# A rebuilt opening for a delta-rule attention and feed-forward kernel on one core

## The chip, the cores and the metric

The kernel runs on one core of a Trainium2 chip. Its engines are TensorE (PE in the profile, with PEld for the loading of its stationary operand), VectorE (DVE), ScalarE (ACT), GpSimd (POOL) and SyncE (SP), which issues most of the transfers. Each engine works through its own instruction stream in order and waits on semaphores for the others. The metric is the device time of one execution in microseconds; lower is better.

## The reference

Two blocks follow each other. The first is a delta-rule attention over 4 batches of 8 heads, 768 positions and 48 dimensions, with normalized keys:

```python
k_n = k / (np.linalg.norm(k, axis=-1, keepdims=True) + 1e-06)
state = np.zeros((B, H, D, D)); y = np.zeros_like(q)
for t in range(S):
    kt, vt, bt = k_n[:, :, t], v[:, :, t], beta[:, :, t, None]
    y[:, :, t] = np.einsum('bhd,bhde->bhe', q[:, :, t], state)
    v_old = np.einsum('bhde,bhd->bhe', state, kt)
    state = state + bt[:, :, :, None] * np.einsum('bhd,bhe->bhde', kt, vt - v_old)
```

Its output, 3072 tokens of 384 numbers, goes through a feed-forward block:

```python
h = x @ w_in                                     # 384 x 2048
g = np.maximum(h, 0.0) + alpha * np.minimum(h, 0.0)
out = g @ w_out                                  # 2048 x 384
```

All is float32.

## The kernel before, in words

The sequence is cut into 12 chunks of 64 positions. A step `n` is one chunk for one pair of batches, so there are 24 steps; steps 0 and 1 are the first chunk. Within a chunk the recurrence becomes a triangular system: a Gram matrix of the keys, weighted by beta, is inverted, and the inverse is applied to the values less what the state already gives. `attention` or the bursts of later steps do this in small matrix products; the feed-forward products of earlier chunks (`ffn_in`, L943, and `ffn_out`) are woven between them by `weave`, which places pieces by their shares. There is no scheduler: the order on every engine is the order of the Python code (`manual_schedule`). PSUM is held as three double banks (`p_pair`), which `ps_big` and `ps_one` hand out in rotation, and two single ones (`p_ffn`, from `ps_ffn`).

The opening is the part from L1528 to the first feed-forward product. It is written out by hand:

- *Loads.* `load_early` brings keys to one of three buffers (`ke`; the fourth step uses `kl`), `load_q`, `load_v` and `load_late` queries, values and a second copy of the keys, all as DMAs on SP's queue but three of the first, which are on ACT's. `fetch_in` issues DMAs of pieces of `w_in`, 512 KB each, to staging space in `w_out` and `space_out`. `begin_in` makes two ACT instructions of each piece (L226, L227) and `convert` two DVE instructions (L236, L241), which turn it into the form that the products read.
- *Key preparation, steps 0 to 3.* `squares` (square on ACT, sum on DVE), `weigh` (root and a small bias on ACT, reciprocal on DVE, two small products on GpSimd, L373 and L374), `flips` (four transpositions on PE, L384, and an eviction to `k_t` by ACT, L410), `grams` (16 small products on PE, L436; two weighted evictions on DVE, L442; and `keep`, which copies half of the rows to `same`: on GpSimd, L485, for steps 0 to 2, and half on DVE, L487, and half on ACT, L489, for step 3). `betas` transposes beta, `slopes` the feed-forward slopes (L310), `queries` multiplies queries by keys (L1417).
- *The first inversion.* `turn_in` transposes `same` into `block` on DVE (L501, 4 instructions). `eliminate_small(0)` then inverts the two 16x16 diagonal blocks of every 32x32 block. It first multiplies `block` by the mask `inside` (L563), which keeps what is strictly above the diagonal; `inside` is made of `ones` (GpSimd, L268 and L269) by a cast on ACT (L1553). Then follow 14 pairs of DVE instructions (L569, L575). `back` transposes the results to `turned` (2 instructions), to `inverse` (4) and to the rest of `turned` (2).
- *Meanwhile* ACT clears tiles (`zeros`, L327 and L329) and begins four weight pieces; PE runs `busy(8)`: eight products of 128x512 (L1407) whose result nobody reads. `busy` takes a PSUM bank and repeats such a product; each shows as two records in the profile.
- *The crossing.* `cross` fills in the off-diagonal 16x16 blocks for a range of blocks: products of `edge` with `turned` (L605), an ACT copy to `half_way` (L610), products with `inverse` (L615 for the upper, L622 for the lower), DVE additions (L629 and L631). In `first_chunk` it runs once over the 16 blocks of steps 0 and 1, with `busy` products inside and behind it.
- *The rest of `first_chunk`.* `scale_v` and `mask` (DVE, L749 and L1425) stand inside the crossing. `place` puts the results into `diag` and `inv` (DVE or ACT, L650 and L654); `between_1` and `between_2` (L721 and L734, with evictions L726 and L741) complete the 64x64 inverse; `solve` (L800, L804), `outputs` (L813, L818) and `to_ffn` (L852, L854) end in the operand of the first L943. Three transpositions of later keys (`flipped`) stand between, and 12 conversion steps.

`second_pair` follows: it does the crossing for steps 2 and 3, in two halves and with products of `ffn_in(0)` between.

Of the kernel before, what the change touches and what calls it, by code (L numbers as in the profile page):

```python
# [32 lines left out]
C = 64  # L33
HB = 32
W_IN_P = 512
BUSY = 8
EARLY = 8
FIRST = 6
LATE = 16
# [4 lines left out]
def kernel(  # L44
# [219 lines left out]
    for t in range(2):  # L264
        nc.gpsimd.tensor_copy(out=above[half(t)], in_=upper[half(t), half(t)])

    ones = work.tile([128, HB, HB], FP32, name="ones", tag="turned", bufs=1)
    nc.gpsimd.memset(ones, 0.0)  # L268
    nc.gpsimd.affine_select(  # L269
        out=ones, in_=ones, compare_op=ALU.is_ge, fill=1.0, base=0,  # L270
        pattern=[[1, HB], [-1, HB]], channel_multiplier=0,
    )
    inside_ = const.tile([128, HB * (HB + 1)], S8, name="inside")
    inside = inside_[:, 0 : HB * HB].rearrange("p (r c) -> p r c", c=HB)

    which = const.tile([128, 2], FP32, name="which")
    nc.gpsimd.memset(which, 0.0)
    for t in range(2):
# [42 lines left out]

    right = [const.tile([128, H + 1, HB], FP32, name=f"right{i}") for i in range(EARLY)]

    def zeros():

        for t in right:
            nc.scalar.memzero(t[:, 0])  # L327
        for t in mid + diag + inv + state:
            nc.scalar.memzero(t)  # L329


    stats, k_t, q_t, a_t = {}, {}, {}, {}
# [97 lines left out]
    def grams(n, p=None):  # L430

        if n >= N:
            return []
        p = region(p, G * C, g=G)
        for g, a, t in quarters():
            nc.tensor.matmul(  # L436
                p[half(t), a, g], k_t[n][dims(a), g, half(t)], k_t[n][dims(a), g, half(t)]
            )
        w = stats[n][1][:, 0:2, :, None].to_broadcast([128, 2, G, HB])

        def weighted(dst, cols):
            nc.vector.tensor_tensor(  # L442
                out=dst.rearrange("p (a g) i -> p a g i", a=2), in0=p[:, :, :, cols], in1=w,
                op=ALU.mult,
            )
# [33 lines left out]
    def keep(n):  # L479

        m, j = n // NJ, n % NJ
        for t in range(2):
            own = slice(64 * t + HB, 64 * t + C)
            if n < FIRST + NJ and n != NJ - 1:
                nc.gpsimd.tensor_copy(out=same[m][own, j], in_=right[n % EARLY][own, 1:])  # L485
            elif n < NJ and t == 0:
                nc.vector.tensor_copy(out=same[m][own, j], in_=right[n % EARLY][own, 1:])  # L487
            else:
                nc.scalar.copy(same[m][own, j], right[n % EARLY][own, 1:])  # L489
        if (m, j) == (0, NJ - 1):  # L490
            for _ in turn_in(m):
                pass
# [98 lines left out]
    def quad(i):  # L591
        return slice(HB * i, HB * i + HB)

    def cross(m, bs, edge, half_way, aside=None):


        def let(b, every):
            if aside is not None and b % every == every - 1:
                aside()

        n = bs.stop - bs.start
        p = ps_one()[:, 0 : n * LB].rearrange("p (b i) -> p b i", i=LB)
        for b in range(n):
            for i in range(4):
                nc.tensor.matmul(  # L605
                    p[quad(i), b], edge[quad(i), bs.start + b],
                    turned[m][quad(i), bs.start + b, 0:LB],
                )
            let(b, 4)
        nc.scalar.copy(half_way[:, bs, 0:LB], p)  # L610
        yield
        p = ps_big()[:, :, 0 : n * LB].rearrange("p w (b i) -> p w b i", i=LB)
        for b in range(n):
            for i in (0, 2):
                nc.tensor.matmul(  # L615
                    p[quad(i), 1, b], inverse[m][quad(i), bs.start + b],
                    half_way[quad(i), bs.start + b, 0:LB],
                )
            let(b, 8)
        for b in range(n):  # L620
            for i in range(4):
                nc.tensor.matmul(  # L622
                    p[quad(i), 0, b], half_way[quad(i), bs.start + b],
                    inverse[m][quad(i), bs.start + b, LB:HB],
                )
            let(b, 4)
        for i in (0, 2):
            y = turned[m][quad(i), bs, 0:LB]
            nc.vector.tensor_tensor(out=y, in0=y, in1=p[quad(i), 1], op=ALU.add)  # L629
# [772 lines left out]
    def busy(n, p=None):  # L1402

        p = ps_one() if p is None else p
        while n > 0:
            x = p[:, 0 : int(512 * min(n, 1))]
            nc.tensor.matmul(  # L1407
                x, ident, k_late[0].rearrange("p h d -> p (h d)")[:, 0 : x.shape[-1]]
            )
            n -= 1  # L1410

# [20 lines left out]
    def first_chunk(mask, convert):  # L1432

        both = (0, 1)
        ahead[0] = n_in

        waits, pause = iter([0.5] * 2), []
        middle = cross(
            0, slice(0, 2 * H), edge, half_way, lambda: pause and busy(next(waits, 0), pause[0])
        )  # L1440
# [11 lines left out]
        place(0, (0,))  # L1452
        place(1, (0,), True)
        for i in both:
            place(i, (1,), True)
            now(between_1(i))
        keys = flipped(NJ, ps_ffn())
        convert(2)
# [6 lines left out]
        norms(NJ)  # L1465
        for i in both:
            now(through_state(i))
            now(solve(i))
        now(flipped(NJ + 1, ps_ffn()))
        for i in both:  # L1470
            now(outputs(i))
        convert(4)
        fetch_in(n_in + 4)
        load_early(NJ + NKE)
        for i in both:
            to_ffn(i, ps_ffn())
        now(flipped(NJ + 2, ps_one()))
        ahead[0] = FT * DM
        convert(4)
        norms(NJ + 1)  # L1480

    def statics(first, last):
# [45 lines left out]
    load_early(NKE)  # L1528
    for n in range(2):
        load_q(n)  # L1530
        load_v(n)
    load_late(0)
    nc.sync.dma_start(out=al_sb, in_=moe_alpha.rearrange("(f p) -> f p", p=128))
    fetch_in(n_in)
    squares(0)
    flips(0, N)
    betas()
    fetch_in(n_in + 2)
    squares(1)
    now(weigh(0))  # L1540
    for n in range(1, NJ):
        if n == 1:
            gram = grams(0)
        flips(n, N)
        if n > 1:
            gram = grams(n - 1)
        now(gram)
        if n + 1 < NJ:
            squares(n + 1)
        now(weigh(n))  # L1550
        load_early(n + NKE)
    now(grams(NJ - 1))
    nc.scalar.copy(inside, ones)  # L1553
    edges(0, edge)
    load_late(1)
    load_v(2)
    slopes()
    for i in range(2):
        flips(N, i)
    for i in range(2):  # L1560
        load_q(i + 2)
    mask = queries()
    nc.scalar.mul(minus, above, -1.0)
    zeros()
# [274 lines left out]
```

## Time and profile before

| | us |
|---|---|
| runs | 658.03, 663.54, 664.56 |
| median | 663.54 |
| span of the profiled execution (the page gives no other time of it) | 658.5 |
| PE busy | 642.4 (98%) |
| DVE busy | 490.4 (74%) |
| ACT busy | 263.9 (40%) |
| POOL busy | 93.4 (14%) |
| first feed-forward product (L943) starts | 48.84 |

Times in the profile count from the first instruction. A line of the timeline has start, length, engine, line, operation, tiles written and read, shapes, the number of instructions merged into it and, in brackets, the idle time of the engine before it and what ended that. The chain that ended last is read in order of time: at each moment the instruction, or the wait ("issue" when the profile shows nothing that was waited for), that the end depended on. A line of the table by stretches gives the stretch, its length, the busy time and number of instructions of PE, PEld, DVE, ACT and POOL, the granted TensorE clock (1.00 is full), the share of DMA engines busy and GB/s.

### The profile page before, as it was taken

The page shows a single profiled execution, that of the slowest core. Times are in us where ns is not written, and L with a number is a line of the kernel's source. Part 1 is how long each engine was busy: PE and PEld are TensorE (multiplying, and loading weights), DVE is VectorE, ACT ScalarE, POOL GpSimd, SP SyncE. Part 2 cuts the span into 40 slices and gives each one's busy share as a digit, 9 for nine tenths or more (in the row PEclk, how much of TensorE's full clock was granted, in tenths as well). Part 3 has the DMA queues.
Part 4 walks back from the last instruction along what each step waited for, and adds up shares of the span by engine and source line. Part 5 has one row for each costly group of instructions (what it writes and reads, how often), then busy time and mean ns, then how long its engine had stood idle before and what let it go on. Part 6 is the DMA issues. An engine that isn't in the chain of part 4 may idle for free.

```text
span 658.5 us, 22123 instructions
## 1 busy us (share of the span) xinstructions
PE 642.4 (98%) x9545; PEld 567.5 (86%) x9545; DVE 490.4 (74%) x1180; ACT 263.9 (40%) x621; POOL 93.4 (14%) x201
## 2 busy tenths in 40 slices
PE   5999999999999999999999999999999999999997
PEld 4477888657788988988988988988989999999997
DVE  3975899977999779658869758868868658567383
ACT  4855755344453443143253242133245245042140
POOL 6000211010000000000000000000035044052260
PEclk9999999999999999999999999999999999999999
DMA  7946745311422122122111111111111210100000
GB/s 124 293 97 158 194 121 148 73 36 37 75 54 50 34 54 38 25 59 41 26 43 33 26 39 36 26 42 33 26 44 32 45 32 2 31 8 2 24 1 25
DMA packets 111154, 37.72 MB, mean 57 GB/s; under 512 B 104224, under 2 KB 107440, under 8 KB 111056
## 3 DMA queue, kind: packets, MB, share of 16 engines
q1 hardware_dynamic: 109184, 35.81, 24.5%
q8 instruction: 75, 1.23, 0.8%
q10 hardware_dynamic: 1872, 0.49, 0.4%
q14 instruction: 23, 0.19, 0.1%
HBM read 31.56 MB, written 4.72 MB: 55 GB/s over the span
## 4 chain that ended last, share of the span: by engine, by line
PE 91%; DVE 5%; ACT 1%; issue 1%; POOL 1%; DMA 1%; SPq 0%; POOLq 0%; ACTq 0%; DVEq 0%
PE p_ffn L943 24%; PE p_ffn L1008 17%; PE p_more L1260 8%; PE p_ffn L986 5%; PE p_more L1176 5%; PE p_ffn L1166 3%; PE p_ffn L1260 3%; PE p_pair L775 2%; PE p_pair L384 2%; PE p_ffn L1171 2%; PE p_pair L686 2%; PE p_pair L800 2%; PE p_pair L813 2%; PE p_pair L1407 2%; PE p_pair L436 2%; PE p_pair L760 1%
## 5 line engine op out<-in xcount | busy, mean ns | idle before, releaser
L943 PE MATMUL p_ffn<-xt,w_in 128*128 128x256 f32 x768 | 176.1, 383 | 0.6 <-DVE act L955 0.5
L943 PEld LDWEIGHTS p_ffn<-xt,w_in 128*128 128x128 f32 x768 | 142.4, 190 | 21.2 <-issue 1.5
L955 DVE SCALAR_TENSOR_TENSOR act<-act,al_t,p_ffn 128x256 f32<-128x256 f32 x112 | 48.7, 476 | 26.5 <-ACT act L953 26.5
L953 ACT ACTIVATE act<-p_ffn 128x512 f32<-128x512 f32 x56 | 33.2, 594 | 79.4 <-PE p_ffn L943 79.2
L534 DVE TENSOR_TENSOR block<-block,prod 128x30 f32<-128x30 f32 (+9 forms) x150 | 49.8, 332 | 5.2
L1200 POOL TENSOR_TENSOR k_t<-k_t 128x128 f32<-128x128 f32 (+1 forms) x48 | 29.3, 610 | 167.1 <-ACT k_t L1195 164.6
L528 DVE TENSOR_TENSOR prod<-block 128x30 f32<-128x30 f32 (+9 forms) x150 | 48.8, 326 | 1.4
L1008 PE MATMUL p_ffn<-w_out,act 128*128 128x192 f32 x288 | 49.6, 328 | 0.0
L854 ACT COPY xt<-p_pair 128x384 f32<-128x384 f32 x22 | 10.4, 478 | 91.1 <-PE p_pair L852 77.3
L1008 PEld LDWEIGHTS p_ffn<-w_out,act 128*128 128x128 f32 x288 | 46.5, 190 | 0.3
L373 POOL TENSOR_TENSOR beta_t<-beta_t,rec 128x8 f32<-128x8 f32 x24 | 6.3, 265 | 283.9 <-DVE rec L371 268.6
L1200 POOL TENSOR_TENSOR block<-block 128x128 f32<-128x128 f32 (+1 forms) x48 | 27.9, 582 | 17.2 <-ACT block L1195 14.7
L1166 PE MATMUL p_ffn<-xt,w_in 128*128 128x256 f32 x96 | 28.7, 381 | 0.5 <-DVE o_sb L1028 0.5
L785 DVE TENSOR_TENSOR r<-v_raw,p_pair 64x192 f32<-64x192 f32 (+1 forms) x66 | 23.3, 353 | 2.3 <-PE p_pair L775 1.2
L698 ACT COPY inv<-p_pair 32x256 f32<-32x256 f32 x40 | 14.4, 361 | 25.0 <-DVE u L804 24.2
L352 DVE TENSOR_REDUCE norm<-ksq 128x8 f32<-128x384 f32 x24 | 13.0, 548 | 14.3 <-ACT ksq L348 14.3
L804 DVE TENSOR_TENSOR u<-p_pair,wgt 128x384 f32<-128x384 f32 x24 | 13.2, 556 | 14.0 <-PE p_pair L686 14.0
L1028 DVE TENSOR_TENSOR o_sb<-u,p_ffn 128x192 f32<-128x192 f32 x24 | 8.0, 352 | 20.4 <-PE p_ffn L1008 20.0
L1214 DVE SCALAR_TENSOR_TENSOR act<-block,al_t,act 128x256 f32<-128x256 f32 x32 | 19.1, 638 | 5.3 <-ACT block L1210 5.2
L764 ACT COPY y<-p_pair 128x384 f32<-128x384 f32 x22 | 10.4, 478 | 30.2 <-PE p_pair L760 26.1
L1260 PE MATMUL p_more<-w_out,act 128*128 128x192 f32 x128 | 21.8, 329 | 0.0
L1195 ACT COPY k_t<-p_more 128x512 f32<-128x512 f32 x16 | 9.4, 585 | 31.1 <-PE p_more L1176 26.4
(228 smaller groups left out, 1422.1 us busy)
## 6 DMA issues: line engine op xcount, KB each, us to landing
w_out<-in_moe_w_in_dram SPq DMA_DIRECT2D x10, 512.0 KB, 5.5
qp<-in_q_dram SPq DMA_DIRECT2D x48, 96.0 KB, 3.0
v_raw<-in_v_dram SPq DMA_DIRECT2D x48, 96.0 KB, 2.9
kl<-in_k_dram SPq DMA_DIRECT2D x96, 48.0 KB, 2.5
out_dram<-o_sb SPq DMA_DIRECT2D x90, 48.0 KB, 1.6
space_out<-in_moe_w_out_dram SPq DMA_DIRECT2D x11, 384.0 KB, 4.1
ke<-in_k_dram SPq DMA_DIRECT2D x43, 96.0 KB, 3.3
w_out<-in_moe_w_out_dram SPq DMA_DIRECT2D x5, 384.0 KB, 4.0
```

What stands on the lines that cost most here:

```text
L528: nc.vector.tensor_tensor(out=prod, in0=r[:, 0:j, j : j + 1].to_broadcast([128, j, n]), in1=r[:, j : j + 1, j + 1 : HB].to_broadcast([128, ...
L534: nc.vector.tensor_tensor(out=r[:, 0:j, j + 1 : HB], in0=r[:, 0:j, j + 1 : HB], in1=prod, op=ALU.add)
L785: nc.vector.tensor_tensor(out=r[to, a], in0=v_in[to, a], in1=p[own, a, :, 0:D], op=ALU.subtract)
L943: nc.tensor.matmul(p_h[:, i], w_in[:, t, (f + i) * 128 : (f + i + 1) * 128], xt[:, t], start=(t == 0), stop=(t == KT - 1),)
L953: nc.scalar.activation(g, p_h, ACT.Relu, scale=-1.0)
L955: nc.vector.scalar_tensor_tensor(out=g[:, i], in0=g[:, i], scalar=al_t[:, f + i : f + i + 1], in1=p_h[:, i], op0=ALU.mult, op1=ALU.add,)
L986: nc.tensor.matmul(p_o[u], gs[f // 2][:, f % 2, u * 128 : (u + 1) * 128], w_out[:, f], start=(f == 0), stop=(f == FT - 1),)
L1008: nc.tensor.matmul(p, x(i), w(i), start=(i == 0), stop=(i == FP - 1))
L1166: nc.tensor.matmul(p[:, f * 256 : f * 256 + 256], w(2, f), xt[:, 2], start=True, stop=False)
L1176: nc.tensor.matmul(q[:, j], a, b, start=True, stop=True)
L1200: nc.gpsimd.tensor_tensor(out=dst, in0=a, in1=b, op=ALU.add)
L1260: nc.tensor.matmul(p, x(i), w(i), start=(i == 0), stop=(i == FP - 1))
```

## The change

Only the opening is changed; from `second_pair` on the code is the same.

- The order of key preparation: weights (`weigh`) of a step come ahead of the evictions of the Gram products of the steps before it, and the transpositions write to the single banks.
- Six products of 128 columns (`WARM`) start PE's stream.
- Key loads 4 to 6 are issued ahead of the weight pieces, the values and late keys behind them.
- `zeros` runs on GpSimd: 12 clears early, 4 more after key preparation.
- The mask `inside` and its product are gone; 15 GpSimd clears of the lower triangles take their place. `keep` uses GpSimd for steps 0 and 1, DVE and ACT for 2 and 3.
- The three later key transpositions move ahead of the crossing, among fillers of 7, 5, 3 and 1 products; between them ACT begins four weight pieces. The filler reads a transposed key tile (112 rows) in place of a late key tile (128 rows).
- The first crossing runs in two halves, without fillers; the upper additions come ahead of the lower products. Value scaling and masks move behind it, and the 12 conversion steps are split 2, 4 and 6.

```diff
-BUSY = 8
+WARM = 6
...
-    def zeros():
-
-        for t in right:
-            nc.scalar.memzero(t[:, 0])
-        for t in mid + diag + inv + state:
-            nc.scalar.memzero(t)
+    def zeros(tiles):
+
+        for t in tiles:
+            nc.gpsimd.memset(t, 0.0)
...
-            if n < FIRST + NJ and n != NJ - 1:
+            if n < 2 or NJ <= n < FIRST + NJ:
...
-        nc.vector.tensor_tensor(out=x, in0=x, in1=own_blocks(inside_), op=ALU.mult)
+        for j in range(1, LB):
+            nc.gpsimd.memset(x[:, :, j, 0:j], 0.0)
...
+        if apart:
+            upper_half()
+            yield
         for b in range(n):
             for i in range(4):
                 nc.tensor.matmul(
                     p[quad(i), 0, b], half_way[quad(i), bs.start + b],
                     inverse[m][quad(i), bs.start + b, LB:HB],
                 )
-            let(b, 4)
...
-        next(middle)
-        pause.append(ps_one())
-        busy(1, pause[0])
+        halves = [cross(0, slice(i * H, i * H + H), edge, half_way, True) for i in both]
+        for h in halves:
+            next(h)
         begin_in(6)
+        for h in halves:
+            next(h)
+        for i in both:
+            place(i, (0,))
+        for h in halves:
+            next(h)
+        for i in both:
+            place(i, (1,), True)
         for i in both:
             scale_v(i)
-            mask(i)
+        for i in both:
+            now(between_1(i))
         convert(2)
         fetch_in(n_in + 3)
-        next(middle)
-        busy(1.25)
...
         for i in both:
             place(i, (2,))
             now(between_2(i))
-        now(keys)
+            mask(i)
...
+    for _ in range(WARM):
+        nc.tensor.matmul(big[0][:, 0, 0:128], ident, ident)
+    zeros([t[:, 0] for t in right] + mid + diag)
+    squared(0)
+    norms(0)
+    now(flipped(0, ps_ffn()))
+    rest = [weigh(0)]
+    squared(1)
+    now(flipped(1, ps_ffn()))
+    load_early(1 + NKE)
+    norms(1)
+    betas()
+    now(rest[0])
+    rest = weigh(1)
+    gram = {0: grams(0)}
+    squared(2)
+    now(rest)
+    norms(2)
+    now(flipped(2, ps_ffn()))
...
+    fetch_in(n_in + 2)
+    now(gram[0][2:])
+    now(gram[1][2:])
+    now(gram[2][:2])
+    gram[3] = grams(3)
+    now(gram[2][2:])
+    now(gram[3][:2])
+    now(gram[3][2:])
...
+    zeros(inv + state)
...
-    busy(BUSY)
-    begin_in(4)
+    for i in range(3):
+        busy(7 - 2 * i)
+        now(flipped(NJ + i, ps_one()))
+        begin_in(i + 2)
+    busy(1)
     for _ in eliminate_small(0):
         pass
```

More of the change, by code (lines that the diff above doesn't have):

```diff
@@ L265 @@
         nc.gpsimd.tensor_copy(out=above[half(t)], in_=upper[half(t), half(t)])
[L267 to L274, printed above, removed]
     which = const.tile([128, 2], FP32, name="which")
@@ L438, in grams @@
             )
-        w = stats[n][1][:, 0:2, :, None].to_broadcast([128, 2, G, HB])
         def weighted(dst, cols):
+            w = stats[n][1][:, 0:2, :, None].to_broadcast([128, 2, G, HB])
             nc.vector.tensor_tensor(
@@ L592, in quad, with cross @@
         return slice(HB * i, HB * i + HB)
[L594 to L599, printed above, removed]
+    def cross(m, bs, edge, half_way, apart=False):
         n = bs.stop - bs.start
@@ L618, in cross, with upper_half @@
                 )
-            let(b, 8)
+        def upper_half():
+            for i in (0, 2):
+                y = turned[m][quad(i), bs, 0:LB]
+                nc.vector.tensor_tensor(out=y, in0=y, in1=p[quad(i), 1], op=ALU.add)
+        if apart:
+            upper_half()
+            yield
         for b in range(n):
@@ L625, in cross @@
                 )
[L626 to L629, printed above, removed]
+        if not apart:
+            upper_half()
         y = inverse[m][:, bs, LB:HB]
@@ L1405, in busy @@
         while n > 0:
-            x = p[:, 0 : int(512 * min(n, 1))]
             nc.tensor.matmul(
-                x, ident, k_late[0].rearrange("p h d -> p (h d)")[:, 0 : x.shape[-1]]
+                p, ident[0:ROWS], k_t[0].rearrange("p g i -> p (g i)")[0:ROWS]
             )
@@ L1435, in first_chunk @@
         ahead[0] = n_in
[L1437 to L1440, printed above, removed]
-        next(middle)
-        pause.append(ps_one())
-        busy(1, pause[0])
-        begin_in(6)
+        halves = [cross(0, slice(i * H, i * H + H), edge, half_way, True) for i in both]
+        for h in halves:
+            next(h)
+        begin_in(6)
+        for h in halves:
[6 more added lines that the diff above has]
+            place(i, (1,), True)
         for i in both:
             scale_v(i)
-            mask(i)
+        for i in both:
+            now(between_1(i))
         convert(2)
         fetch_in(n_in + 3)
-        next(middle)
-        busy(1.25)
[L1452 to L1458, printed above, removed]
         for i in both:
@@ L1461, in first_chunk @@
             now(between_2(i))
-        now(keys)
+            mask(i)
         for i in both:
             squared(NJ + i)
-        norms(NJ)
         for i in both:
@@ L1468, in first_chunk @@
             now(solve(i))
-        now(flipped(NJ + 1, ps_ffn()))
         for i in both:
@@ L1473, in first_chunk @@
         fetch_in(n_in + 4)
+        norms(NJ)
         load_early(NJ + NKE)
@@ L1476, in first_chunk @@
             to_ffn(i, ps_ffn())
-        now(flipped(NJ + 2, ps_one()))
         ahead[0] = FT * DM
-        convert(4)
+        convert(6)
         norms(NJ + 1)
@@ L1530 @@
         load_q(n)
-        load_v(n)
-    load_late(0)
[L1533 to L1554, printed above, removed]
+    nc.sync.dma_start(out=al_sb, in_=moe_alpha.rearrange("(f p) -> f p", p=128))
+    for _ in range(WARM):
[17 more added lines that the diff above has]
+    now(flipped(2, ps_ffn()))
+    load_early(2 + NKE)
+    load_early(3 + NKE)
+    rest = weigh(2)
+    gram[1] = grams(1)
+    squared(3)
+    now(gram[0][:2])
+    now(rest)
+    norms(3)
+    now(flipped(3, ps_ffn()))
+    rest = weigh(3)
+    gram[2] = grams(2)
+    now(gram[1][:2])
+    now(rest)
+    fetch_in(n_in + 2)
[6 more added lines that the diff above has]
+    now(gram[3][2:])
+    for i in range(2):
+        flips(N, i)
+    for n in range(2):
+        load_v(n)
+    edges(0, edge)
+    mask = queries()
+    slopes()
+    nc.scalar.mul(minus, above, -1.0)
+    zeros(inv + state)
+    load_late(0)
     load_late(1)
     load_v(2)
-    slopes()
-    for i in range(2):
-        flips(N, i)
     for i in range(2):
         load_q(i + 2)
-    mask = queries()
-    nc.scalar.mul(minus, above, -1.0)
-    zeros()
+    begin_in(1)
     for i in range(2):
         place(i, (3,))
-    busy(BUSY)
-    begin_in(4)
+    for i in range(3):
[3 more added lines that the diff above has]
+    busy(1)
     for _ in eliminate_small(0):
```

## The prediction

> **What bounds the kernel now.** I read four views in this order: busy time by stretches, the chain that ended last, VectorE's and TensorE's timelines around the hand-over, and TensorE's filler line by itself. First the stretches (length; then busy us and count of PE, PEld, DVE, ACT, POOL; granted clock, DMA share, GB/s):
>
> ```profile
> 4.42:19.51 15.09, 11.16 (x160) 8.87 (x160) 9.14 (x25) 8.16 (x24) 6.66 (x23) 1.00 0.91 185
> 19.51:30.68 11.17, 11.17 (x80) 5.56 (x80) 9.95 (x35) 10.96 (x30) 0.71 (x3) 1.00 1.02 310
> 30.68:48.84 18.16, 17.19 (x638) 13.84 (x637) 13.33 (x32) 9.58 (x21) 0.00 (x0) 1.00 0.43 91
> 80.00:640.00 560.00, 558.23 (x7799) 499.33 (x7798) 428.80 (x1019) 212.17 (x499) 76.95 (x144) 1.00 0.20 43
> ```
>
> From 80 to 640 us TensorE is idle for 1.8 us in all, so the rest follows the first feed-forward product (L943, at 48.84) one for one: the change is worth what it moves that moment, and what it does to the next few microseconds. The chain up to there:
>
> ```profile
> 16.03 0.42 DVE same L442
> 16.45 0.34 DVE right L442
> 16.81 0.41 ACT same L489
> 17.25 1.03 ACT inside L1553
> 18.29 0.62 ACT sums L589
> 18.91 0.07 ACT al_t L311
> 18.98 0.48 ACT beside L412
> 19.46 0.04 issue
> 19.51 1.98 PE p_ffn L1417 x57
> 21.49 9.26 PE p_pair L1407 x16
> ```
>
> (Line numbers are those of before: L605, L615, L622, L721, L734, L943 become L589, L598, L613, L710, L723, L932.) Key preparation runs to 17.2, ACT evictions hold the queries to 19.5, and then eight filler matmuls, not the inversion, lead to the crossing (L605, 30.68). VectorE shows that the fillers were the later: the two transposes that L605 needs ended by 29.36, and `inverse` by 31.4, when L605 was still running.
>
> ```profile
> 28.27 1.09 DVE L501 STREAM_TRANSPOSE turned<-block 128x256 f32<-128x256 f32 x2
> 29.20 2.21 DVE L501 STREAM_TRANSPOSE inverse<-block 128x256 f32<-128x256 f32 x4
> ```
>
> Last, two single filler passes:
>
> ```profile
> 23.29 1.06 PE L1407 MATMUL p_pair<-kl,ident 128*128 128x512 f32 x1
> 29.73 0.59 PE L1407 MATMUL p_pair<-kl,ident 128*128 128x512 f32 x1
> ```
>
> The granted clock says 1.00 in both places, but passes get short once in the run: up to 25.8 one starts every 0.86 us, later every 0.43 (16 passes over 9.26 us: five slow and eleven fast make 9.0). The fast ones came 6.3 us after TensorE began at 19.51 to work without a pause. A filler is two passes: 1.72 slow, 0.86 fast.
>
> **The change, part by part.** *Key preparation.* The cast `inside` (1.03 on ACT) and the product with it (L563, 0.69 on DVE) go; squares, roots and evictions are reordered so that gram products follow a key later. In the new order a key costs ACT a square, an eviction, a root and a bias, 0.43+0.50+0.22+0.17 = 1.3, plus waits for DVE's sum (0.47) and TensorE's transposes (0.87): about 2.2 a key. Key 1's square starts at 6.1 as before, key 3's bias ends about 12.2; reciprocal 0.2, the two GpSimd products 0.52, DVE's two weighted copies and own-rows copy 0.95, ACT's copy 0.4: the block transposes start at 14.7 (now 17.25). Two keys' rows are now copied on GpSimd after the last weights, 4 x 0.41 from 13.0, done by 14.7: level with DVE and ACT. If they come later, the whole inversion is queued behind that wait, but 5 us of it are free, as the fillers show next.
>
> *Clears.* Twelve on GpSimd stand ahead of the first weights. The trace has 0.53 for 128x512 and between 0.10 (128x2) and 0.20 (128x128) for the small: 4 x 0.5 + 8 x 0.10 to 0.20 = 2.8 to 3.6, against 2.2 saved there (`ones`). GpSimd was through at 7.40; now 8.0 to 8.8. The first reciprocal ends about 9.0, so I take zero, with 0 and 0.5 as bounds. The 15 triangle clears lie between 0.10 and 0.31 each (L580), 1.5 to 4.7 us, beside 7.9 us of elimination; only the final transposes wait for them. I take 0.15, cost zero. ACT loses 5.0 us of clears (19.98 to 24.99) that ran beside the fillers: nothing.
>
> *SP's queue.* Order is now q1, slopes, keys 4 to 6, eight weight pieces, v0, v1, late keys. Slopes move from 13.8 to about 8.1, so TensorE's 1.68 us wait for them goes (though it was only partly on the chain). The key loads wait for transposes and squares of keys 1 and 2, about 10; weights then issue from about 12.5 (now 14.46). ACT's first conversion, now at 25.83, moves up to 16.6 and stands there until its piece lands, 5.5 after issue by the table of DMA issues, at 18. Queued behind it are the weight copies and the eviction of the first key transposition; that one is due at 22, and the fillers of the third group wait for it. Only a piece later than 22 would cost anything. The values v0 and v1 and the late keys now wait on SP for weight pieces to land; eight pieces took 0.5 MB each at some 400 GB/s, so the last is down by 26 and the values by 28, and their scaling comes after 36. Cost zero.
>
> *Fillers.* Queries can start at 15.2 (after ACT's two row copies and one beside-copy), the slope transposition at 16.2, fillers at 16.3. They now are 7+5+3+1 = 16, with three key transpositions of 0.45 between: 16 x 0.86 + 1.35 = 15.1. So the crossing starts at 31.4, though VectorE has `turned` at 14.7+2.3+7.9+1.1 = 26.0 and `inverse` at 28.1. The opening is rebuilt to be ready five microseconds sooner and gives them to filler: 31.4 against 30.68, a loss of 0.7.
>
> Whether they run fast is the open price. New early matmuls (six of 128 columns from 1.5, 0.43 each, done before keys arrive at 4.42) cost nothing. From key 1's landing (6.1) the new order keeps TensorE busy to about 14.4; at the trace's 6.3 us of unbroken work the passes turn fast at 12.4, ahead of the fillers. Bounds: all fast, 15.1; or counting starts with the queries at 15.2 and passes turn fast only at 21.5, which adds half of 21.5 - 15.2, 3.1 us. I take the fast end, since the stretch from 6.1 is longer than the one that sufficed.
>
> The Trainium skill (TensorE: Matmul & The Clock Gate, What's actually happening) says the clock starts at half rate and is released after one busy free-running window of about 3.4 us. The trace's halving fits; by that rule release comes 3.4 to 6.8 us after unbroken work begins, so 9.5 to 12.9 here, the same sum, and an added 1.7 to 3.4 us if the gate did not count small products.
>
> *Crossing to first product*, now 18.16. Out: fillers 1.05+0.63+0.63+1.35 = 3.66 and three key transpositions of 0.58, 0.58, 0.44 = 1.60: 12.9 left. In: ACT now has a fourth and two more weight conversions (1.3 each) around the two half copies, so the first `diag` place is queued behind them: TensorE stands about 1.0 ahead of L721, where now it stood 0.22. Masks and value scaling come behind the crossing on DVE; a mask (0.66) lies between L730 and the last `u`, 0.4 exposed. Copies of the first half overlap the second half's products, which gives back about 0.6. Sum 13.5: 31.4 + 13.5 = 44.9, against 48.84: 3.9 earlier. Bounds: 12.3 if no wait is exposed, 15.0 if all of DVE's masks and scaling (2.1) is.
>
> The Trainium skill (GPSIMD Engine Reference, Specifications) says GpSimd shares its SBUF interfaces with VectorE and collides with instructions of two SBUF inputs, which the elimination's are: a rule against this change. The trace has the two side by side only for half a microsecond (L580 at 19.58). If each clear stopped VectorE for its length, `turned` came at 28, still before the fillers end; the sum is the same.
>
> *After it.* DVE now has six conversion steps and two sums (4.2 us) between the last `u` and the first state update, so the second half of the next L605 waits about 1.2. In its place the trace has this:
>
> ```profile
> 53.91 0.71 PE L605 MATMUL p_pair<-turned,sums 32*32 32x16 f32 x62 [1.59 <-issue]
> ```
>
> I take the two as equal; both standing would cost 1.2, neither would gain 1.6. The sum stays -3.9. All good ends together are -5.1 - 1.6 = -6.7; all bad ones 0.5 + 3.1 + 15.0 - 13.5 + 1.2 - 3.9 = +2.4. So 658.5 - 3.9 = 654.6 in the profiled execution's own terms. Its span is all that the page gives of its time, and it stands level with the fastest of the three runs (658.03, 663.54, 664.56), 5.0 below the median. I set the sum against the median: 663.5 - 3.9 = **659.6**.
>
> **The rivals.** *Fillers start slow* (the early small products do not count): the crossing starts 0.7+3.1 late at most, half of that in the middle; L943 at 46.4 to 48.0, time 661.1 to 662.7, say 662. For it: short passes came only under big matmuls. Against: pauses of 0.36 and more broke every earlier stretch.
>
> *More is gained*: nothing in the trace says why two of three runs are over 5 us above the third. If that lies in the opening (late loads, passes that turn fast late), the new order, with weights sooner and work denser, ends it: 654.6. Against: no run shown places it there.
>
> *Slower: bursts without fillers stall.* In the second pair, which has none between, TensorE stood 1.59 with "issue" inside L605, a wait that no semaphore explains; in L721 it stood 0.42. The new crossing strings six such bursts together. Each stall of 1.59 that is not under another wait costs its length; three (4.8) undo the gain and decide, six (9.5) give 663.5 + 5.6 = 669. Against: the second pair's other bursts (L615, L622) show none.
>
> **How the numbers follow.** Forecast 0.48, slow fillers 0.22, more gained 0.20, stalls 0.10. The forecast's own range is 657 to 663. To hold 8 in 10, the range goes down to 654.0, just past the middle of the third case, and up to 664.5, past the slow fillers into the bad ends; most of the stalls and the far half of the third case, 2 in 10, are left out. Within 1% is 656.9 to 670.2, about what a measurement of this kernel can tell from no change. Faster: the third case and a tenth of the forecast, 0.25; slower: two thirds of the stalls, 0.07; the same: 0.68.
>
> **What would show it.** Block transposes at 14.7; fillers from 16.3, each pass 0.43 apart; the crossing (L589) at 31.4 with `turned` ready over 4 us earlier, so TensorE, not DVE, in the chain there; L932 first at 44.9. Fillers 0.86 apart at 17 mean the second case; "issue" stalls in L589 to L613, the last. I am wrong if the crossing waits for VectorE or if L943's stream after 80 us is no longer dense.

## The result, and the profile after

The changed kernel takes 667.5 us (median of 16 runs, 662.93 to 670.13), the kernel before 662.94 (16 runs, 658.03 to 671.68): a ratio of 1.0084, 95% interval 1.0056 to 1.0112. It is 0.84% or 5.6 us slower, where 659.6 was forecast. The profiled execution after took 668.09, its span is 666.4, 7.9 longer than the span before. I read it in stretches first (columns as in the prediction: length; busy us and count of PE, PEld, DVE, ACT, POOL; granted clock, DMA share, GB/s):

```profile
4.42:18.61 14.19, 13.07 (x224) 10.66 (x223) 10.06 (x28) 7.97 (x21) 8.52 (x43) 1.00 1.01 191
18.61:36.51 17.90, 17.90 (x45) 8.13 (x45) 10.69 (x35) 6.85 (x16) 0.82 (x8) 1.00 0.79 225
36.51:57.11 20.60, 16.36 (x615) 15.44 (x615) 9.87 (x26) 9.01 (x21) 0.00 (x0) 0.67 0.22 50
88.00:648.00 560.00, 558.65 (x7802) 499.62 (x7801) 429.49 (x1020) 212.83 (x500) 76.86 (x144) 1.00 0.20 43
```

The long stretch is as dense as before (1.35 us idle in 560), so the loss again stands whole at the first feed-forward product: 57.11 against 48.84, 8.27 later. Two stretches hold it. The fillers end, and the crossing begins, at 36.51 instead of 30.68 (+5.83); from there to L932 it takes 20.60 instead of 18.16 (+2.44), with 0.67 as the mean granted clock, where it was 1.00. The chain of waits of after shows the same place:

```profile
18.68 8.85 PE p_pair L1395 x14
27.53 0.44 PE p_pair L373 x4
27.97 4.29 PE p_pair L1395 x10
...
39.86 1.45 issue
41.30 1.90 PE p_pair L613 x128
43.20 1.95 issue
45.16 3.62 PE p_pair L710 x64
```

Fillers (L1395) lead into the crossing again, and in it stand two long waits that no engine and no transfer ends. VectorE was through long before the crossing began, in its timeline:

```profile
16.07 2.28 DVE L489 STREAM_TRANSPOSE block<-same 128x256 f32<-128x256 f32 x4
...
26.27 1.06 DVE L489 STREAM_TRANSPOSE turned<-block 128x256 f32<-128x256 f32 x2
27.20 2.21 DVE L489 STREAM_TRANSPOSE inverse<-block 128x256 f32<-128x256 f32 x4
```

`turned` is ready at 27.3, nine microseconds ahead of L589 and two ahead of its counterpart before (29.36).

**The clock.** The profile's clock record begins at 23.97 after (at 25.88 before), and the tables count the time ahead of it as full. It was not: filler passes start 0.85 us apart until 23.90 and 0.43 from 24.37 on. In narrow stretches the granted clock is 0.50 from 41.03 to 54.69:

```profile
37.62:41.03 3.41, 1.54 (x99) 1.39 (x90) 1.12 (x4) 2.93 (x7) 0.00 (x0) 1.00 0.43 79
41.03:44.44 3.41, 1.90 (x128) 1.79 (x128) 1.46 (x5) 0.68 (x2) 0.00 (x0) 0.50 0.02 5
44.44:54.69 10.25, 9.53 (x221) 9.43 (x224) 4.94 (x13) 2.37 (x6) 0.00 (x0) 0.50 0.19 55
54.69:58.10 3.41, 3.27 (x87) 2.43 (x82) 3.31 (x7) 2.90 (x6) 0.00 (x0) 1.00 0.14 19
```

TensorE is busy for 1.54 of the 3.41 us up to 41.03, and then its clock is halved for 13.65. The same products are dear there. Before:

```profile
35.54 1.38 PE L622 MATMUL p_pair<-inverse,act 32*32 32x16 f32 x128
41.58 2.00 PE L734 MATMUL p_pair<-diag,mid 64*64 64x32 f32 x62
```

After:

```profile
41.30 1.90 PE L613 MATMUL p_pair<-inverse,act 32*32 32x16 f32 x128 [2.15 <-issue]
45.16 3.62 PE L710 MATMUL p_pair<-diag,right 64*64 64x32 f32 x64 [1.95 <-issue]
48.56 3.52 PE L723 MATMUL p_pair<-diag,mid 64*64 64x32 f32 x62
```

**The "issue" waits.** I numbered TensorE's records by start: PE and PEld together, with the semaphore records between them, which the page does not count. In the 16 traces of this study the waits named "issue" stand at numbers that are 194 above a multiple of 256: 706, 962, 1218 and so on, whatever product that is (43 waits of more than 0.15 us; three others, of 0.34, 0.16 and 0.16, stand elsewhere). The page of after (queue, kind: packets, MB, share) has the partner of this:

```profile
q8 instruction: 75, 1.23, 0.8%
```

75 packets for 2 x 9563 products and loads and 139 semaphore records are 257 records and 16.4 KB each. I call such a packet a block. When TensorE passed a block's end, in us:

| number | 706 | 962 | 1218 | 1474 | 1730 |
|---|---|---|---|---|---|
| before | 31.70 | 35.83 (+4.1) | 39.94 (+4.1, 0.42 of it waiting) | 44.25 (+4.3, 0.20) | 48.38 (+4.1) |
| after | 37.05 | 41.30 (+4.3, 2.15) | 45.05 (+3.8, 1.95) | 51.80 (+6.8) | 55.12 (+3.3) |

The trace has the time of each packet, and it ties the waits to them. In after one landed at 39.84, and TensorE went on at 41.30; the next landed at 43.65, and it went on at 45.05. All 43 waits ended 1.20 to 1.84 us after the landing of such a packet. So these are waits for instructions; that the length of a whole burst follows from them is for the experiments to show.

The crossing before, which looks 95% busy, passes a block every 4.1 to 4.3 us. My theory for the experiments: instructions reach TensorE no faster than about 4 us per 256 in such a stretch, so that fillers in it were nearly free, and what is taken out of it comes back as an "issue" wait; the waits then halve the clock; and the 16 fillers ahead are plain delay. The rivals: the fillers ahead are needed, or the loss in the crossing is only missing cover for the clock.

### The profile page after: what moved, and what is told of

The parts are those of the page before. It is cut to its first block, busy times and chain, and to the rows that moved or that the text cites. A ratio compares the mean times of both kernels' runs of the same rounds, so it can differ in the third digit from the quotient of the medians.

```text
span 666.4 us, 22162 instructions
## 1 busy us (share of the span) xinstructions
PE 653.2 (98%) x9563; PEld 575.9 (86%) x9563; DVE 491.0 (74%) x1182; ACT 259.4 (39%) x607; POOL 95.0 (14%) x228
## 3 DMA queue, kind: packets, MB, share of 16 engines
q1 hardware_dynamic: 109184, 35.81, 24.7%
## 4 chain that ended last, share of the span: by engine, by line
PE 91%; DVE 4%; ACT 1%; DMA 1%; issue 1%; SPq 0%; DVEq 0%
PE p_ffn L932 23%; PE p_ffn L997 17%; PE p_more L1249 8%; PE p_ffn L975 5%; PE p_more L1165 4%; PE p_ffn L1155 3%; PE p_ffn L1249 3%; PE p_pair L373 3%; PE p_pair L1395 2%; PE p_pair L764 2%; PE p_ffn L1160 2%; PE p_pair L675 2%; PE p_pair L789 2%; PE p_pair L802 2%; PE p_pair L425 2%; PE p_pair L749 1%
## 5 line engine op out<-in xcount | busy, mean ns | idle before, releaser
L932 PE MATMUL p_ffn<-xt,w_in 128*128 128x256 f32 x768 | 176.1, 383 | 0.6 <-DVE act L944 0.5
L932 PEld LDWEIGHTS p_ffn<-xt,w_in 128*128 128x128 f32 x768 | 142.4, 190 | 21.2 <-issue 1.5
L1189 POOL TENSOR_TENSOR block<-block 128x128 f32<-128x128 f32 (+1 forms) x48 | 27.6, 575 | 16.7 <-ACT block L1184 14.2
L793 DVE TENSOR_TENSOR u<-p_pair,wgt 128x384 f32<-128x384 f32 x24 | 13.2, 555 | 14.2 <-PE p_pair L675 14.0
L341 DVE TENSOR_REDUCE norm<-ksq 128x8 f32<-128x384 f32 x24 | 12.9, 544 | 12.8 <-ACT ksq L337 12.8
L643 ACT ACTIVATE inv<-inverse,which 128x256 f32<-128x256 f32 x44 | 21.6, 504 | 0.3
```

The costliest lines, as they stand in the source:

```text
L932: nc.tensor.matmul(p_h[:, i], w_in[:, t, (f + i) * 128 : (f + i + 1) * 128], xt[:, t], start=(t == 0), stop=(t == KT - 1),)
L1189: nc.gpsimd.tensor_tensor(out=dst, in0=a, in1=b, op=ALU.add)
```

## The experiments

A ratio is to the kernel before on the same chip (its medians: 662.95 beside e1 to e4, 662.37 beside e5 to e8, 661.19 beside e9 and e10, 669.28 beside e11 and e12). "Stretch" is first crossing product to first feed-forward product.

**Fewer fillers ahead.** Two edits to the changed kernel, six fillers (e2) and none (e12), and a third (e11, the closed opening) with the six, and two small products, spread over TensorE's idle places.

```diff
-        busy(7 - 2 * i)
+        busy((3, 1, 1)[i])
```

> The changed kernel with 3, 1, 1 and 1 fillers ahead of the crossing in place of 7, 5, 3 and 1. Theory: the 16 fillers alone hold the crossing at 36.5, while VectorE has the first part of `turned` at 27.3 and `inverse` at 29.4; with 6 it starts at 27.7 to 28.5, 8 to 8.8 us sooner. The bare crossing stays, with its two stalls and the halved clock, so the whole gain passes on: 658.5 to 659.5. Rival (GpSimd): the clears slow or delay the inversion, so that the crossing, freed of fillers, waits for VectorE until 30 or later: 661 or more.

Measured: 657.77 us (10 runs, 656.86 to 665.4), ratio 0.996 [0.992, 1.0001]: 9.7 below the changed kernel. L589 starts at 25.55, waiting for VectorE, 11.0 earlier; the stretch is 19.9, with waits of 0.85 and 1.00 at numbers 962 and 1218. The first theory holds, with 0.7 us more gained than it forecast: ten fillers were delay. In the profiled run some 2 of the 11.0 us are the clock's and not the fillers': here it was full from 5.81 to 16.05, and VectorE began to write `turned` at 24.34, in after at 26.27.

```diff
-        busy(7 - 2 * i)
...
-    busy(1)
```

> The changed kernel with no filler at all ahead of the crossing (the six-filler kernel less its six). Theory (the fillers' only worth is the clock at which the crossing begins): L589 still at 25 to 26, since VectorE sets it; TensorE idle for most of 16 to 25, the clock at 0.50 when the crossing begins and through all of it, so 21 to 22.5 us to the first feed-forward product instead of 19.9, and 659 to 661. Rival (the crossing goes by the instruction supply alone, whose floor hides the clock): 19.5 to 20.2 us and 657 to 658.5.

Measured: 659.96 (10 runs), 0.9926 [0.9884, 0.9969]. The clock was half through nearly all of the stretch, and yet it took 19.88 us:

```profile
27.78 1.90 PE L589 MATMUL p_pair<-turned,sums 32*32 32x16 f32 x128 [6.45 <-DVE turned L489]
29.77 1.89 PE L598 MATMUL p_pair<-act,inverse 32*32 32x16 f32 x64
...
36.37 2.05 PE L710 MATMUL p_pair<-diag,right 64*64 64x32 f32 x33 [0.56 <-issue]
```

The rival's length, then: slower products fit into the time that the blocks need anyway, and the "issue" waits at 962 and 1218 shrink to 0.24 and 0.56 (a third, of 0.53, stands at 1730). The time is the theory's, for another reason: L589 came at 27.78 and not 25.5, since the opening ran at half clock until 20.8.

```diff
+    for _ in range(2):
+        nc.tensor.matmul(big[0][:, 0, 0:128], ident, ident)
     rest = [weigh(0)]
...
+    busy(2)
     mask = queries()
...
-        busy(7 - 2 * i)
+        busy(1)
```

> The six-filler kernel with TensorE's idle places in the opening closed: two small products behind the first key's transpositions (0.66 us idle there) and two of the six fillers ahead of the queries (1.69 us idle there). Theory (the clock is lost and won in whole windows of 3.41 us, and where the windows fall changes from run to run, so that only an opening without idle places has the full clock every time): 1.00 from 5 to 8.5 us on without a fall until the crossing; L589 at 25.5, set by VectorE; 656 to 657.5, and a narrower spread than the six-filler kernel's 656.9 to 665.4. Rival (the opening is VectorE's, and the clock there does not matter): 657 to 658.5 with the same spread.

Measured: 658.16 (4 runs, 657.58 to 658.52), 0.9896 [0.9777, 1.0015]. The spread of these four runs was narrow, as expected, and the clock held from 5.47, but it was lost as the crossing began; the median is the rival's:

```profile
5.47:25.95 20.48, 15.82 (x292) 9.97 (x294) 17.54 (x58) 15.21 (x37) 8.29 (x41) 1.00 1.01 269
25.95:46.43 20.48, 17.91 (x571) 16.78 (x563) 12.77 (x32) 7.80 (x18) 0.00 (x0) 0.50 0.53 98
```

**Fillers out of the old crossing alone** (e4; the kernel before):

```diff
-        middle = cross(
-            0, slice(0, 2 * H), edge, half_way, lambda: pause and busy(next(waits, 0), pause[0])
-        )
+        middle = cross(0, slice(0, 2 * H), edge, half_way)
...
-        busy(1, pause[0])
+        ps_one()
...
-        busy(1.25)
+        ps_one()
```

> The kernel before with the fillers in and behind its crossing taken out (3.66 us by their rows). Theory: they lay under the supply of instructions, 16.7 us for the four blocks from 31.7 to 48.4, so nothing is gained: the same time if the clock stays full, 2 to 5 us more if the idle time halves it, 662.5 to 668. Rival (the reckoning of the prediction): they are work on the path, and without them the kernel takes 3 to 3.7 us less, 659 to 660.

Measured: 665.36 (10 runs), 1.0067 [1.0035, 1.0099]. Taking out 3.66 us of fillers made the stretch 21.5 instead of 18.2. A wait of 0.80 stands at number 962, one of 1.5 for ACT's `diag` ahead of L721, and the clock is halved from 35.47 to 49.12. My sum, which took 3.66 off, is refuted here by itself.

**256 records more in the old crossing** (e7; L605 issues each product twice):

```diff
+                for _ in range(2 if n > H else 1):
+                    nc.tensor.matmul(
```

> The kernel before, every product of L605 in its first crossing issued twice with the same result: 64 more products, 256 more instructions. Theory (supply): one more block, 3.8 to 4.3 us more to L943 in place of the 1.3 that their rows cost. Rival (sum of work): 1.3 us more. Either way a clock halved by lower use would show in the record and add to it.

Measured: 673.12 (4 runs), 1.0161 [1.0083, 1.024]. Products that the row prices at 1.4 us made this line 6.2 us longer:

```profile
30.78 1.32 PE L606 MATMUL p_pair<-turned,sums 32*32 32x16 f32 x106
...
34.04 1.50 PE L606 MATMUL p_pair<-turned,sums 32*32 32x16 f32 x128 [1.94 <-issue]
...
37.77 0.61 PE L606 MATMUL p_pair<-turned,sums 32*32 32x16 f32 x22 [2.22 <-issue]
```

From one wait's end to the other's, 3.73 us, lie 128 product records with their loads, which is 256 records. The supply shows most plainly here. Beyond this line the clock, halved from 36.09 to 59.99, adds more than the theory had: the stretch is 32.4, 14.2 longer than before, where 3.8 to 4.3 were forecast.

**Do the waits belong to numbers or to products?** To the six-filler kernel, small products added at the very start (e9):

```diff
+    for _ in range(95):
+        nc.tensor.matmul(big[0][0:HB, 0, 0:LB], ident[0:HB, 0:HB], ident[0:HB, 0:LB])
```

> The kernel with six fillers, and 95 products of 32x32 by 16 columns more in TensorE's idle time before the first key lands (190 more instruction records ahead of everything). Theory of the instruction supply: the stalls stay at the same instruction numbers (194 above a multiple of 256), so they leave the products where they stood (0.85 us in L613, 1.00 in L710) and come 190 records earlier in the work; four block ends instead of five lie between the first crossing product (then number 725) and the first feed-forward product, and that stretch takes 17.0 to 18.5 us instead of 19.9: the time falls 1.5 to 3 below the six-filler kernel, to 655 to 656.5. Rival (the stalls belong to the products, through something that the trace does not name): they stay in L613 and L710 at some 0.9 each, and the time is the same, 657 to 658.5. A halved clock from 29.7 on, as in the six-filler kernel, is expected in both.

Measured: 668.4 (4 runs), 1.0127 [1.0084, 1.017]. I had miscounted: each product makes four records (two passes, each with its load), so the crossing began at number 916, and they took 8.0 us, more than the idle time, so the whole opening came later. The time tells nothing. The places do:

```profile
38.22 1.30 PE L598 MATMUL p_pair<-act,inverse 32*32 32x16 f32 x42 [0.99 <-issue]
39.48 1.36 PE L613 MATMUL p_pair<-inverse,act 32*32 32x16 f32 x86
41.96 0.82 PE L613 MATMUL p_pair<-inverse,act 32*32 32x16 f32 x42 [1.12 <-issue]
```

These are numbers 1218 and 1474. The wait at 1218 was in L710 and is now in L598: it went with the number, not with the product. The added products show something of the clock too: it was halved at 8.34, after a window in which they kept TensorE busy without a pause.

```profile
4.93:8.34 3.41, 3.41 (x112) 3.41 (x111) 0.55 (x1) 0.18 (x1) 2.52 (x13) 1.00 1.38 168
```

**Fewer records in the crossing.** In the changed kernel (e13) and in the one with the closed opening (e14), four products of L589 and of L613 were issued as one:

```diff
-            for i in range(4):
-                nc.tensor.matmul(
-                    p[quad(i), b], edge[quad(i), bs.start + b],
-                    turned[m][quad(i), bs.start + b, 0:LB],
-                )
+            nc.tensor.matmul(p[:, b], few(edge, b), turned[m][quad(0), bs.start + b, 0:LB])
```

> The changed kernel, with the four 32x32 products per block of L589 and L613 of the first pair issued as one product of 32 rows and 128 columns: 32 products in place of 128 in each line, 384 instruction records fewer (this leaves out three quarters of the crossing's sum and computes other values in its place, so only its time is read). The products that go cost 1.0 us (L589) and 1.4 us (L613). Theory of the instruction supply: the stretch L589 to L932, 20.6 us now with five block ends (706 to 1730) in it, has three, its 872 records at some 4 us per 256 make 13.6, and with the waits for VectorE it takes 14.5 to 16.5; at most one issue wait over 1 us. Rival (clock and products set the length): 20.6 - 2.4 = 18.2, between 17.8 and 19, with both issue waits of about 2 still there. Time 668 less what the stretch loses.

> The same edit in the six-filler kernel with the closed opening, whose stretch took 21.3 us with issue waits of 1.08 and 1.20 and a half clock throughout. Supply: 14.5 to 16.5 us, at half clock too, and some 652 us. Rival (clock and products): 18.5 to 19.5 us and 655.5.

Measured: stretches of 24.07 and 26.6 us (one run each, of 676.47 and 673.97), outside all four expectations. The merged product is dear:

```profile
36.83 3.74 PE L590 MATMUL p_pair<-turned,sums 32*128 32x16 f32 x32
...
42.01 6.98 PE L617 MATMUL p_pair<-inverse,act 32*128 32x16 f32 x32 [0.23 <-DVE turned L610]
```

The kernels slow down as wholes too, since later crossings of the same kind are merged with the first. What the first one can still tell: with the clock halved nearly as before (41.44 to 58.5), both long "issue" waits are gone, and 24.07 less the two lines is 13.35, while after's 20.60 less its two lines (1.44, 1.90) and its two waits (4.10) is 13.16. The waits do not come with the halved clock, nor with the divided crossing; they go when the blocks come further apart (here 11.2 and 5.1 us). Nor does the halved clock come with the waits, as my theory had it: here it fell without one, after a window in which TensorE had no pause.

```profile
38.03:41.44 3.41, 3.41 (x81) 3.38 (x82) 0.16 (x1) 1.09 (x3) 0.00 (x0) 1.00 0.25 49
```

**The same fillers in smaller pieces** (e6; the kernel before, 32 of 128 columns for 8 of 512):

```diff
-    busy(BUSY)
+    p = ps_one()
+    for _ in range(4 * BUSY):
+        nc.tensor.matmul(
+            p[:, 0:128], ident, k_late[0].rearrange("p h d -> p (h d)")[:, 0:128]
+        )
```

> The kernel before, its eight fillers of 512 columns ahead of the crossing split into 32 of 128 columns: the same columns, 96 more instructions. Theory (supply): the boundary at instruction 706, now about 1 us into L605, falls among the fillers, where its successor has time to arrive, so the crossing gets its first 250 instructions without a wait and L943 comes 1.5 to 3 us sooner. Rival (sum of work): only the instructions' own cost counts, 0 to 1.5 us more.

Measured: 666.34 (10 runs), 1.0064 [1.0034, 1.0093], the wrong sign. I had the crossing's first number wrong: it is 490 before, and 96 more leave 706 inside L605. The ends of the blocks moved to other products: a wait of 2.63 stands at number 1218, now in L622, the clock is halved from 40.16 to 53.81, and the stretch is 25.8.

**Cover put back into the divided crossing.** Two fillers ahead of the first L613 and two behind L613 (e1), the same with six fillers ahead (e3); two behind L589 and two behind L613 (e5), the same with six ahead (e8). The edit of e1 and e3:

```diff
+        busy(2, big[0][:, 0])
         for i in both:
             place(i, (0,))
         for h in halves:
             next(h)
+        busy(2, big[0][:, 0])
         for i in both:
             place(i, (1,), True)
```

In e5 and e8 the first of the two lines stands ahead of `begin_in(6)`, behind L589.

> The changed kernel with four fillers put back into its crossing: two ahead of the lower products, two ahead of L710. Theory (supply and clock): TensorE's instructions come in blocks of 256 that start no less than some 4 us apart, which left it idle 2.15 and 1.95 us here, and idleness halved its clock for 13.65 us. The fillers fill the idle time, the clock stays full, and from the first crossing product to the first L932 it takes 17 to 18 us in place of 20.6: about 3 us faster than the changed kernel, 664 to 665. Rival (sum of work): the stalls are waits for ScalarE and VectorE and the length is work, so four fillers add up to 3.4 us: 668 to 671.

> Both edits: 6 fillers ahead of the crossing, four in it. Theory: the two effects are separate and add, 8 to 9 us and 3 us: first L932 at 45 to 46.5, 655.5 to 657, which beats the kernel before by about 1%. Rival (sum of work): the four inner fillers are paid for, so this is 1 to 3 us slower than the kernel with 6 fillers alone.

> The changed kernel again with four fillers in the crossing, but earlier: two between L589 and L598, two after L613. In the run with inner fillers they stood behind the point where TensorE stopped (1.94 us, at its instruction 962, as 1.6 to 2.2 us in other kernels at 962, 1218, 1986 and 2498, always 194 more than a multiple of 256), so they ran after the stall and at half clock. Theory (supply): a new block of 256 instructions comes some 4 us after the one before was begun; fillers ahead of the boundary cover that time. So no stall over 1 us, the clock is not halved after 30 us, and 17.5 to 18.5 us from L589 to L932 (20.6 in the changed kernel): 664 to 665.5. Rival (sum of work): 3.4 us of fillers are added, 668 to 671.

> The changed kernel with 6 fillers ahead of the crossing (3, 1, 1, 1) and four in it, placed ahead of the boundaries: two after L589, two after L613. Theory: crossing from 27.5 to 28.5, 17.5 to 18.5 us to L932 at full clock, first L932 at 45 to 47: 655 to 657.5, at or below the 657.8 of the kernel with 6 fillers and a bare crossing. Rival (sum of work): 3 us more than that kernel, 661.

| | time | ratio | stretch |
|---|---|---|---|
| e1 | 668.27 (4 runs) | 1.0103 [1.0037, 1.0168] | 19.97 |
| e3 | 660.55 (10) | 0.9975 [0.9941, 1.0008] | 21.4 |
| e5 | 670.73 (4) | 1.0127 [1.0058, 1.0196] | 24.6 |
| e8 | 660.17 (10) | 0.9965 [0.9915, 1.0014] | 23.5 |

All four times are near the rival's: no cover gained time. Its reason, waits for ScalarE and VectorE, does not hold where the wait is at a block's end. In e1 the wait stands ahead of the fillers (their first product is number 962), and they ran at half clock:

```profile
40.90 3.46 PE L1395 MATMUL p_pair<-k_t,ident 112*128 112x512 f32 x4 [2.06 <-issue]
```

Its mean clock over the stretch was 0.91, against after's 0.67, and the stretch, with four fillers more in it, was 0.6 shorter.

**The new preparation with the old crossing** (e10), six fillers ahead, `cross` and `first_chunk` as they stood:

```diff
-        busy(7 - 2 * i)
-        now(flipped(NJ + i, ps_one()))
-        begin_in(i + 2)
-    busy(1)
+    busy(6)
+    begin_in(4)
```

> The changed kernel's preparation with six fillers, and then the crossing of the kernel before as it stood: undivided, with its pauses, its fillers and its three key transpositions. Theory (the preparation is a gain, and the old crossing keeps the full clock): L605 at 25.5, set by VectorE; 18.2 us to the first feed-forward product, at a clock of 1.00 through the crossing; first product at 43.7, 5.1 before the kernel before, and a time of 656 to 658 beside a before of about 663. Rival (the old crossing's 18.2 us holds only after a long run of fillers, and the clock halves here too): 19.5 to 22 us for the crossing, first product at 45.5 to 47.5, and a time of 659 to 661.5, no better than the six-filler kernel with the divided crossing (657.8).

Measured: 662.43 (10 runs, 655.87 to 669.55), 1.0018 [0.9976, 1.0059]. Nearer the rival, and worse than it: the crossing starts at 27.36 and takes 20.7, with the clock halved from 37.78 to 44.60, and the first product comes at 48.09. The old crossing's 18.2 is not a property of its order alone. Its ten runs had mean clocks of 0.969 to 1.000, and the one at 1.000 took 655.87.

## Why the prediction was wrong

*Bound and place: right.* The first feed-forward product sets the time (8.27 there, 7.9 in the span), TensorE and not VectorE leads to the crossing, and GpSimd's clears cost nothing: the elimination took 7.78 us against 7.80, though only 1.0 us of it lay beside clears (0.15 before). So the Trainium skill's warning (GPSIMD Engine Reference, Specifications) of contention for the shared SBUF interfaces is hardly tested here. Weights issued at 12.90 and `turned` at 27.3 came close to 12.5 and 26.0.

*The first step that failed: "So 16 x 0.86 + 1.35 = 15.1", with "I take the fast end".* The block transposes started at 16.07, not 14.7; the queries at 16.48, not 15.2, and they and the slopes took until 18.61, not 16.3. Then the passes were slow until 23.97, so fillers and transpositions took 17.9 us. Crossing at 36.51 instead of 31.4: 5.1 of the miss. My second case (slow fillers) came true, for 2.8. The other 2.3 go with the same clock: the block transposes started at 14.1 to 14.2 in the four runs with this preparation and a full clock that began at 5.25 to 5.81 (e2, e5, e8, e11), and at 15.9 to 16.4 in those where it came at 20.8 to 24.7. (My sum for this step also had slips: 1.3, 0.47 and 0.87 are 2.6 a key and not 2.2, and the terms behind 12.2 make 14.3 and not 14.7.) In the six-filler run the full clock began at 5.81 and in this one at 23.97, with the same opening work: what I argued about, whether the early products count, is decided in each run by where the windows fall.

*The second, and the larger: "Out: fillers ... 3.66 and three key transpositions ... 12.9 left", and the sum 13.5.* It took 20.60, 7.1 more. I counted a busy TensorE as work that can be taken out. The fillers and transpositions lay in time in which the next instructions were not there: without fillers the stretch got longer (e4), and 256 records more cost 6.2 where their row said 1.4 (e7). After's 20.60 in rows: two waits of 4.10 at block ends; half clock for L613, L710, L723 and L789 to L802, about 4.1 more than the same products before; what is left, 12.4, is near my sum. The two are not simply additive: at half clock nearly throughout, the stretch is also 19.9 (e12).

*The rival "bursts without fillers stall"*, at 0.10, had the mechanism and too small a price: I took 1.59 per wait and three waits to undo the gain; two of 2.15 and 1.95 came, and the halved clock, which I had in no case. The range's bad ends (fillers +3.1, crossing 15.0) were too near in both steps, and both came together.

*The base.* I set the sum against the median and said that nothing in the trace tells why runs of one kernel differ by 5 us. In the kernel before, the clock goes with it. Of its runs, beside the experiments, 23 with a mean granted clock of 0.999 or 1.000 took 659.6 in the mean, 11 with 0.994 or 0.995 took 663.4, and 7 with 0.991 or 0.992 took 665.7 (one run of 1654 us is left out). The profiled execution that I costed had 0.999, the changed kernel's 16 runs 0.974 to 0.990. This fits that the two traces differ by 7.9 and the medians by 5.6: typical runs before lose some clock as well. It is read from runs as they came, not from an experiment that sets the clock, and the mean has its limits: it counts the time ahead of the first clock record as full, and among the changed kernel's own runs the fastest (662.93) had 0.981 and the slowest (670.13) 0.990.

*The clock rule.* The Trainium skill (TensorE: Matmul & The Clock Gate, What's actually happening) has a free-running window of about 3.4 us; the changes at 23.97, 41.03 and 54.69 agree, being 5.00 and 4.00 times 3.413 apart. It lets the clock fall after an idle window; here it fell after a window with 1.54 of 3.41 us busy, and in e9 and e13 after windows without a pause, filled with 32-row products of 16 columns, so the measurement says that no idle window is needed. It lets a busy window release the clock; here the release at 23.97 came after two without a pause.

*Left open.* How the 7.1 divides between supply and clock; no traced run had a crossing without fillers at full clock throughout. A rough estimate from the table of block ends: with before's 4.3 in place of 6.8 for the block from 1218 to 1474, after's stretch would be some 18.2, which leaves 2.4 to the clock and 4.7 to the supply. What share of which products keeps the clock was not settled, and with it why four kernels with cover lost it anyway. The six-filler kernel and the one with the closed opening (657.8 and 658.2) are the best versions here: ten below the changed kernel, and below the kernel before by an amount that depends on its clock (ratios 0.996 and 0.9896, both intervals just touching 1; that of e12, 0.9926, lies wholly below 1, beside a kernel before of 669.28).

## What to carry to other kernels

Before taking filler or moved work out of a burst of small products, number the instructions: if the burst passes 256 of them every 4 us, its length is the supply's, and a busy engine there is not a sum that can be shortened. Fill an engine only up to the moment at which its successor's operand is ready; ten fillers past that moment cost 9.7 us here. And ask of a profiled execution what clock it had, before setting a forecast against a median of others.

## What the runs showed of the hardware

- TensorE's instructions come in blocks of 256 records (75 packets of 16.4 KB for 19265 records, semaphore records included), and the waits end 1.20 to 1.84 us after a packet's landing. Block ends in the first crossing are about 4 us apart when products press (3.3 the least; 2.6 once in a later pair, after a block of 7.1), and the wait, up to 2.63 us, stands at the same numbers whatever the kernel.
- The granted clock is halved for whole multiples of 3.41 us (3.41, 6.83, 10.24, 13.65, 17.07, 20.48 and 23.89 in the first 60 us); seven of the 16 traces have one of 13.65 there. It fell after windows of 3.41 us that TensorE spent wholly on 32-row products of 16 columns (e9 at 8.34, e13 at 41.44), so a busy TensorE alone does not hold it.
- One pass (a product is two) of 32 rows with a 128-column stationary operand and 16 columns took 117 ns at full clock and 218 at half; four 32x32 passes of the same columns took 42 and 59 together (1.33 us and 1.90 us for 128).
